# Eight transfers of the first steady unit on another queue, in an mLSTM and MLP kernel

## The chip, the cores and the metric

The kernel runs on one core of a Trainium2 chip. A core has five engines that run side by side and meet at semaphores: TensorE (PE in the profile; PEld is its weight load), VectorE (DVE), ScalarE (ACT), GpSimd (POOL) and SyncE (SP). SP, ACT and POOL can also start DMA transfers; each of them issues its own in the order of its instructions. The metric is the time of one execution in device microseconds (us).

## The reference, cut to what matters

```python
def _attn_ref(q, k, v, i_gate, f_gate, o_gate):          # B, H, S, D = 4, 8, 768, 40
    for t in range(S):
        m_new = np.maximum(f_gate[:, :, t] + m, i_gate[:, :, t])
        f_stab = np.exp(f_gate[:, :, t] + m - m_new)
        i_stab = np.exp(i_gate[:, :, t] - m_new)
        C = f_stab * C + i_stab * einsum('bhd,bhe->bhde', vt, kt)
        n = f_stab * n + i_stab * kt
        h_tilde = einsum('bhde,bhe->bhd', C, qt)
        denom = np.maximum(np.abs(einsum('bhd,bhd->bh', n, qt)), 1.0)
        y[:, :, t] = sigmoid(o_gate[:, :, t]) * h_tilde / denom
...
def _moe_ref(x, w_in, w_out):                             # x: 3072 x 320, d_ff 2048
    h = x @ w_in
    return (h - np.tanh(h)) @ w_out
```

A recurrent cell (mLSTM) with a state per head is followed by a two-layer MLP whose inner function is h - tanh(h). All is float32.

## The kernel before, in words

The sequence of 768 steps is cut into 6 chunks of 128. One chunk of one of the 4 batches is a unit, so there are 24 units, and two units make a group of 256 tokens for the MLP. The 2048 inner columns of the MLP are taken in 8 pairs of 128-wide blocks. A work item is one or two pairs of one group: first the products with `w_in` into the PSUM tiles `ph_up`, then the inner function on ACT and DVE (tiles `z`, `q`, `gt`), then the products with `w_out`. In the steady part these are done with seven products instead of eight on 2 by 2 blocks (`up_in_seven`, line 1220, `down_seven`, line 1029), which need sums and differences of blocks made beforehand: `sums_in` and `part` from `w_in` (`sum_w_in`, line 1196), `wT` from `w_out` (`sums_of_weights`, line 1005), `s` from `gt`. When a group's products with `w_out` are done, DVE puts the PSUM tiles `pS` together into the output tile `ob` (`put_together`, line 1072).

Units 0 to 5 are placed by a planner. Units 6 to 23 (`PLANNED = 6`, line 296) are the steady ones. Each runs as a chain over several engines: PE makes the scores (`ps`) and then the turned result `pT` (`block_turned`); ACT and DVE bring `pT` into `zt` (`turn_back`, line 905); four transfers write `zt` to device memory (`h_rows`), and four read it back in another order (`z_in`), the second four after the first have landed. Then DVE makes the denominator (`den`), scales by the output gate and has `y` (`ys`, `gate_turned`, line 928); DVE transposes it to `yt`, four transfers write it out (`y_rows`) and three on POOL's queue read it into `xT`, the MLP's input for that unit's group (`turn_by_store`, line 825). Of unit 6 the four `y_rows` transfers are on POOL's queue, of the other units on SP's.

Every engine's instructions are pinned to the order in which the program emits them (`class Pinned`, line 96), and a DMA is one of its issuing engine's instructions: whatever stands behind a waiting DMA waits too. What stands where is decided by the main loop: `spread_over` puts steps at fractional positions of the items (`START + x`), and `merge` (line 1375) lays them between PE's products. SP's queue also carries the copies of the recurrent states (`in_halves`, line 849, emitted ahead of the steady part) and the loads of the coming units (`load_unit`, line 355: `kz`, `qz`, `v`, `k`, `o`).

Of the kernel before, what the change touches and what calls it, by code (L numbers as in the profile page):

```python
# [79 lines left out]
def kernel(  # L80
# [33 lines left out]
    V, A, SP, G = Pinned(nc.vector), Pinned(nc.scalar), Pinned(nc.sync), Pinned(nc.gpsimd)  # L114
# [181 lines left out]
    PLANNED, LEFT = 6, 3  # L296
# [345 lines left out]
    part = [parts_of[n // GT][:, n % GT] for n in range(FIRST * GT)]  # L642
# [179 lines left out]
    BLOCK = 32  # L822
# [82 lines left out]
    def turn_back(n):  # L905


        t = un[n]
        both = att.tile([128, 2, HH * L // BLOCK, BLOCK], FP, name="zt", tag="P", bufs=4)
        zt, added = both[:, 0], both[:, 1].rearrange("p b i -> p (b i)")  # L910
        flat = zt.rearrange("p b i -> p (b i)")
        banks_of = [x.rearrange("p g t -> p (g t)") for x in t["turned"]]
        A.copy(out=added[:, HALF:], in_=banks_of[1][:, HALF:])
        V.transpose(flat[:, 0:HALF], banks_of[0][:, 0:HALF])
        sums = [x.rearrange("p (i t) -> p i t", i=2)[:, :, HALF:] for x in (added, banks_of[0])]
        V.tensor_tensor(out=sums[0], in0=sums[1], in1=sums[0], op=OP.add)
        V.transpose(flat[:, HALF:], added[:, HALF:])
        rows = dram.tile([2, 2, HH, L, BLOCK], FP, name="h_rows", tag=f"h_rows{n % 4}")
        for a in range(128 // BLOCK):
            half, low = divmod(a, 2)  # L920
            SP.dma_start(out=rows[low, half].rearrange("g (b k) i -> k (g b) i", k=BLOCK), in_=zt[a * BLOCK:(a + 1) * BLOCK])
        t["z"] = att.tile([L, 2, H, BLOCK], FP, name="z_in", tag="P", bufs=4)
        for i in range(4):
            part = slice(i * BLOCK, (i + 1) * BLOCK)
            SP.dma_start(out=t["z"][part].rearrange("t a h i -> t (a h) i"),
                         in_=rows.rearrange("a c g t i -> t (a c g) i")[part])

    def gate_turned(n):
# [215 lines left out]
    def up(some, shrink, quarters=False):  # L1144

        n = len(some)
        ph = [ps_h.tile([128, 2, TG], FP, name="ph_up", tag=f"ph{i}") for i in range(2)]

        def product(i, x, j):
            g, p = some[x]  # L1150
            f = 2 * p + i
            if j < NK:
                col = 2 * j + i
                lhs, rhs = w_in[:, p, col * 128:(col + 1) * 128], xT[slot_of(g)][:, j, :]
            else:
                rows = slice(i * HALF, (i + 1) * HALF)
                lhs, rhs = w_in[rows, p, 2 * NK * 128:], xT[slot_of(g)][rows, j, :]
            T.matmul(ph[i][:, x, :], lhs, rhs, start=(x == 0 and j == 0), stop=(j == NK), skip_group_check=True)

        def quarter(i, x, c):  # L1160
            g, p = some[x]
            rows, cols, first = slice(i * HALF, (i + 1) * HALF), slice(c * HALF, (c + 1) * HALF), 2 * NK * 128 + c * HALF
            T.matmul(ph[i][cols, x, :], w_in[rows, p, first:first + HALF], xT[slot_of(g)][rows, NK, :],
                     start=False, stop=True, skip_group_check=True)

        full = [(0.43, lambda i=i, x=x, j=j: product(i, x, j)) for i in range(2) for x in range(n) for j in range(NK)]
        if quarters:
            rest = [lambda i=i, x=x, c=c: quarter(i, x, c) for x in range(n) for c in range(2) for i in range(2)]
        else:
            rest = [lambda i=i, x=x: product(i, x, NK) for x in range(n) for i in range(2)]  # L1170
        return full, (rest, [lambda: shrink(some, ph)])
# [24 lines left out]
    def sum_w_in(p, E=V):  # L1196

        a11, a21, a12, a22 = (w_in[:, p, i * 128:(i + 1) * 128] for i in range(4))
        t = sums_in_of(p)
        both = w_in[:, p, 0:4 * 128].rearrange("p (j f) -> p j f", j=4)  # L1200
        return [lambda: E.tensor_tensor(out=t[:, 0:4:2], in0=both[:, 1:4:2], in1=both[:, 0:2], op=OP.subtract),
                lambda: E.tensor_tensor(out=t[:, 1], in0=a22, in1=t[:, 0], op=OP.subtract),
                lambda: E.tensor_tensor(out=t[:, 3], in0=a12, in1=t[:, 1], op=OP.subtract)]
# [196 lines left out]
    while sum(map(len, items)) < len(pairs):  # L1400
        x = sum(map(len, items))
# [64 lines left out]
    of_tokens, of_states, exponentials, rows = {}, {}, [], []  # L1466
# [252 lines left out]
    def spread_over(steps, x0, x1):  # L1719

        for i, (cost, step) in enumerate(steps):
            at = x0 + i * (x1 - x0) / len(steps)
            work[int(at)].append((at, cost, step))
# [9 lines left out]
    for i, slot in enumerate(slots):  # L1733
        x0, x1 = (START + max(0, 2 * j - 1) for j in (i, i + 1))
        begins[x0].append((slot, x0, x1))
    for p, x in enumerate((4.05, 6.05, 8.05, 2.02, 0.5, 0.8, 1.1, 1.4)):
        spread_over([(0.0, lambda step=step: step()) for step in sum_w_in(p, G)], START + x, START + x + 0.25)
    late = (4, 0.0, V), (5, 0.04, G), (6, 0.95, V), (7, 0.3, G)
    for p, x, E in (*late, *((p, x, G) for p, x in zip(order_of(FIRST)[:2] + order_of(FIRST)[-2:], (1.5, 1.75, 6.6, 7.5)))):
# [12 lines left out]
    for x in range(START, len(items) + LAG):  # L1752
# [17 lines left out]
        if x < len(items):  # L1770
            some = tuple(run[:2] for run in items[x])
            turned = [(1.9, lambda n=n: [block_turned(n), Clock.later("turned", 1.2, lambda: [turn_back(n), n + B < NU and keep_halves(n)])]) for n in scored]
            if x < len(items) - 1:
                plain = x < START + PLAIN
                if plain:
                    full, rest = up(some, shrink(x), bool(new[:1]))
                    dense = full[:4] + turned + full[4:]
                else:
                    stages, rest = up_in_seven(x, some)
                    dense = stages[0] + take(BETWEEN) + (turned if new else []) + stages[1] + take(BETWEEN) + stages[2]  # L1780
            else:
                dense, rest = up(some, shrink(x), bool(scored or new[:1]))
            dense.append((0.6 + 0.9 * len(new[:1]), lambda: halves(rest, *(crossed_scores(n) for n in new[:1]))))
            if x == len(items) - 1 or not new and not plain:
                dense += turned
# [96 lines left out]
    def shrink_any(ph):  # L1882
        z = mlp.tile([128, 2, TG], FP, name="z", tag="z")
        q = mlp.tile([128, 2, TG], FP, name="q", tag="q")
        t, big = (att.tile([128, 2, TG], FP, name=name, tag="P", bufs=4) for name in ("t", "big"))
        gt = mlp.tile([128, 2, TG], FP, name="gt", tag="gt", bufs=4)
        A.activation(out=z, in_=ph, func=AF.Square)
        A.activation(out=t, in_=ph, func=AF.Tanh)
        A.activation(out=q, in_=z, func=AF.Square, bias=square)
        A.activation(out=big, in_=z, func=AF.Relu, bias=border)  # L1890
        V.scalar_tensor_tensor(out=gt, in0=ph, scalar=lead, in1=z, op0=OP.mult, op1=OP.mult)
        V.tensor_tensor(out=t, in0=ph, in1=t, op=OP.subtract)
        V.scalar_tensor_tensor(out=gt, in0=z, scalar=root, in1=gt, op0=OP.add, op1=OP.mult)
        V.scalar_tensor_tensor(out=gt, in0=q, scalar=rest, in1=gt, op0=OP.add, op1=OP.mult)
        V.copy_predicated(gt, big.bitcast(I32), t)
        return gt

    with tc.If(loaded[0] > 0):
# [21 lines left out]
        for g in range(NG):  # L1920
# [19 lines left out]
            for p0 in range(0, NP, 2):  # L1940
                gts = []
                full, half = up(((g, p0), (g, p0 + 1)), lambda _, phs: gts.extend(shrink_any(ph) for ph in phs))
# [53 lines left out]
```

## Time and profile before

| | |
|---|---|
| Median of 3 timed runs | 501.25 us (500.5 to 503.71) |
| The profiled execution | 506.16 us, span 504.2 us |
| PE busy in the span | 489.6 us (97%) |
| DVE busy | 411.7 us (82%) |
| ACT busy | 268.8 us (53%) |
| POOL busy | 120.0 us (24%) |
| DVE idle until `z_in` landed, over the whole run | 8.3 us in 5 waits |

All times in what follows count from the start of the span. The page cuts the span into 40 slices, of 12.6 us each; a digit is the busy share in tenths. In rows of the order of time a row can be several instructions of one kind (x4); the first number is the start of the first, the second the time until the end of the last, and in brackets stands how long the engine had been idle and what ended that. Matmul rows overlap with the next, since matmuls are pipelined.

### The profile page before, as it was taken

The numbers are of one execution on the slowest core, as the hardware profiler recorded it, in microseconds if no ns is written. First come the engines' busy times: TensorE is split into PE (matmuls) and PEld (weight loads), VectorE is DVE, ScalarE is ACT, GpSimd is POOL, SyncE is SP. The second block draws the span as 40 slices with busy tenths as digits, with TensorE's granted clock in tenths as the row PEclk, the third lists the DMA queues.
The fourth block names the chain that finished last, engine by engine and source line by source line (L and its number), as shares of the span: only waits on it lengthen the run. The fifth ranks groups of instructions, "written<-read, shape, count | busy, mean of one in ns | idle before, by whom it ended". The sixth has DMA issues, their size and how long they took to land.

```text
span 504.2 us, 13823 instructions
## 1 busy us (share of the span) xinstructions
PE 489.6 (97%) x5208; PEld 438.3 (87%) x5208; DVE 411.7 (82%) x966; ACT 268.8 (53%) x729; POOL 120.0 (24%) x240
## 2 busy tenths in 40 slices
PE   9999999999699999999999999999999999999994
PEld 5778887779599989999999999999999999998984
DVE  4499898995699998887888888888888888885762
ACT  2788998534155445445455455455455464455540
POOL 4552343860134332102103103102102102111000
PEclk9999999999989999999999999999999999999998
DMA  7994395314255444454454344444344343320001
GB/s 226 276 268 128 106 145 151 95 41 89 46 146 119 89 113 80 96 134 89 94 123 98 82 121 85 96 119 96 76 111 101 66 114 59 59 62 10 27 2 31
DMA packets 144044, 51.26 MB, mean 102 GB/s; under 512 B 124004, under 2 KB 136484, under 8 KB 143972
## 3 DMA queue, kind: packets, MB, share of 16 engines
q1 hardware_dynamic: 135308, 31.70, 31.1%
q0 software_dynamic: 5184, 14.52, 9.6%
q10 hardware_dynamic: 3480, 4.10, 2.4%
q8 instruction: 43, 0.70, 0.6%
q14 instruction: 29, 0.24, 0.1%
HBM read 38.40 MB, written 11.60 MB: 99 GB/s over the span
## 4 chain that ended last, share of the span: by engine, by line
PE 81%; DVE 10%; DMA 3%; issue 2%; SPq 2%; ACT 1%; DVEq 0%; ACTq 0%
PE ph_up L129 34%; PE pS L129 29%; PE ps L129 4%; PE po L129 3%; PE pT L129 3%; PE awake L129 3%; PE ph L129 2%; DVE gt L106 2%; PE pc L129 2%; SPq L106 2%; DMA h_rows<-zt 1%; DMA z_in<-h_rows 1%; DVE s L106 1%; DMA y_rows<-yt 1%; DVE w_e L106 1%
## 5 line engine op out<-in xcount | busy, mean ns | idle before, releaser
L129 PE MATMUL ph_up<-xT,w_in 64*64 64x256 f32 (+3 forms) x1324 | 155.2, 349 | 0.2 <-DVE gt L106 0.2
L129 PEld LDWEIGHTS ph_up<-xT,w_in 128*128 128x128 f32 (+2 forms) x1324 | 114.2, 162 | 17.7 <-issue 3.3
L106 ACT ACTIVATE z<-ph_up 128x256 f32<-128x256 f32 (+1 forms) x98 | 40.7, 417 | 102.6 <-PE ph_up L129 80.8
L106 ACT COPY ph_up<-ph_up 128x256 f32<-128x256 f32 x117 | 41.8, 357 | 93.6 <-PE ph_up L129 62.9
L106 POOL DMA_DIRECT2D xT<-y_rows x54 | 31.7, 592 | 238.5 <-DMA y_rows<-yt 238.5
L129 PE MATMUL pS<-wT,s 128*128 128x160 f32 x504 | 87.2, 301 | 0.0
L129 PEld LDWEIGHTS pS<-wT,s 128*128 128x128 f32 x504 | 73.4, 192 | 0.3 <-issue 0.3
L106 ACT ACTIVATE q<-z,tiny 128x512 f32<-128x512 f32 (+1 forms) x98 | 68.9, 713 | 2.5
L106 DVE SCALAR_TENSOR_TENSOR gt<-q,gt 128x512 f32<-128x512 f32 (+1 forms) x98 | 66.6, 686 | 3.9 <-ACT q L106 1.5
L106 DVE TENSOR_TENSOR both<-ph_up,cs 128x256 f32<-128x256 f32 x78 | 32.7, 422 | 35.7 <-PE ph_up L129 30.4
L129 PE MATMUL pS<-w_out,gt 128*128 128x160 f32 x336 | 58.1, 316 | 3.2 <-DVE ob L106 3.2
L129 PEld LDWEIGHTS pS<-w_out,gt 128*128 128x128 f32 x336 | 47.8, 193 | 7.7 <-DVE ob L106 3.3
L129 PE MATMUL ph_up<-xT,sums_in 128*128 128x128 f32 x336 | 52.1, 278 | 1.0 <-DVE gt L106 1.0
L129 PEld LDWEIGHTS ph_up<-xT,sums_in 128*128 128x128 f32 x336 | 45.9, 193 | 1.9 <-issue 1.4
L129 PE MATMUL ph_up<-xT,part 128*128 128x128 f32 x288 | 44.7, 278 | 0.3 <-DVE gt L106 0.3
L106 DVE SCALAR_TENSOR_TENSOR gt<-ph_up,z 128x256 f32<-128x256 f32 (+1 forms) x98 | 41.2, 458 | 2.3 <-ACT z L106 2.2
L129 PEld LDWEIGHTS ph_up<-xT,part 128*128 128x128 f32 x288 | 38.9, 191 | 2.0 <-ACT ph_up L106 1.5
L106 DVE TENSOR_TENSOR s<-gt 128x256 f32<-128x256 f32 x84 | 34.1, 446 | 1.4
L129 PE MATMUL pS<-wT,gt 128*128 128x160 f32 x168 | 30.2, 303 | 0.0
L129 PE MATMUL pS<-w_out,s 128*128 128x160 f32 x168 | 29.7, 299 | 0.0
L129 PEld LDWEIGHTS ps<-qz,kz 40*64 40x64 f32 (+1 forms) x672 | 23.6, 148 | 5.6 <-issue 1.8
L129 PE MATMUL po<-w_out,gt 128*128 128x320 f32 x96 | 27.9, 439 | 0.0
(139 smaller groups left out, 747.7 us busy)
## 6 DMA issues: line engine op xcount, KB each, us to landing
w<-in_moe_w_out POOLq DMA_DIRECT2D x8, 640.0 KB, 5.4
h_rows<-zt SPq DMA_DIRECT2D x72, 64.0 KB
z_in<-h_rows SPq DMA_DIRECT2D x72, 64.0 KB
w<-in_moe_w_in POOLq DMA_DIRECT2D x16, 256.0 KB, 5.1
kz<-in_kT SPq DMA_DIRECT2D x48, 80.0 KB
o<-in_o_gate SPq DMA_DIRECT2D x24, 160.0 KB
qz<-in_qT SPq DMA_DIRECT2D x44, 80.0 KB
out<-ob ACTq DMA_DIRECT2D x11, 320.0 KB
```

The source lines that it names most:

```text
L106: i = method(*args, **kwargs)
L129: return cls.keep(nc.tensor.matmul(*args, **kwargs))
```

## The change

Two things change. In `turn_back` the eight transfers of unit 6, `h_rows` and `z_in`, are issued by POOL instead of SP. And the three sums of `w_in` for pair 7 start at position 1.3 instead of 1.4, so that they come ahead of these transfers in POOL's order.

```diff
         V.transpose(flat[:, HALF:], added[:, HALF:])
+        queue = G if n == PLANNED else SP
         rows = dram.tile([2, 2, HH, L, BLOCK], FP, name="h_rows", tag=f"h_rows{n % 4}")
         for a in range(128 // BLOCK):
             half, low = divmod(a, 2)
-            SP.dma_start(out=rows[low, half].rearrange("g (b k) i -> k (g b) i", k=BLOCK), in_=zt[a * BLOCK:(a + 1) * BLOCK])
+            queue.dma_start(out=rows[low, half].rearrange("g (b k) i -> k (g b) i", k=BLOCK), in_=zt[a * BLOCK:(a + 1) * BLOCK])
         t["z"] = att.tile([L, 2, H, BLOCK], FP, name="z_in", tag="P", bufs=4)
         for i in range(4):
             part = slice(i * BLOCK, (i + 1) * BLOCK)
-            SP.dma_start(out=t["z"][part].rearrange("t a h i -> t (a h) i"),
+            queue.dma_start(out=t["z"][part].rearrange("t a h i -> t (a h) i"),
                          in_=rows.rearrange("a c g t i -> t (a c g) i")[part])
...
-    for p, x in enumerate((4.05, 6.05, 8.05, 2.02, 0.5, 0.8, 1.1, 1.4)):
+    for p, x in enumerate((4.05, 6.05, 8.05, 2.02, 0.5, 0.8, 1.1, 1.3)):
         spread_over([(0.0, lambda step=step: step()) for step in sum_w_in(p, G)], START + x, START + x + 0.25)
```

On SP, behind the loads of unit 8 (`o` is the last of them) and ahead of those of unit 9 (which begin with `kz`), the transfers of unit 6 (numbers 1304 and 1309) and of unit 7 (1499 and 1504) follow each other. This is the difference in SP's order, with the tiles' numbers:

```order
 L106 DMA k_1236<-in_k 64x160 x2
 L106 DMA o_1241<-in_o_gate 128x320
-L106 DMA h_rows_1304<-zt_1299 32x16x32 x4
-L106 DMA z_in_1309<-h_rows_1304 32x16x32 x4
 L106 DMA h_rows_1499<-zt_1494 32x16x32 x4
 L106 DMA z_in_1504<-h_rows_1499 32x16x32 x4
```

Unit 6's eight transfers have left; unit 7's stand directly behind the loads of unit 8.

On POOL, at the end of the sums of `w_in` for pairs 4 to 7 (`sums_in`), this stood before; `wT` are the sums of `w_out` for pairs 0 and 3, `part_148` those of `w_in` for pair 3, and `vs` is the clearing of unit 7's spare columns:

```order
L106 MEMSET vs 128x23
L106 TENSOR_TENSOR sums_in<-w_in,sums_in 128x128
L106 TENSOR_TENSOR wT<-w_out 128x160
L106 TENSOR_TENSOR sums_in<-w_in,sums_in 128x128
L106 TENSOR_TENSOR wT<-w_out,wT 128x160
...
L106 TENSOR_TENSOR wT<-w_out,wT 128x160
L106 TENSOR_TENSOR part_148<-w_in 128x2x128
L106 TENSOR_TENSOR part_148<-w_in,part_148 128x128 x2
L106 DMA y_rows<-yt 32x10x32 x4
```

And this stands there now:

```order
L106 TENSOR_TENSOR sums_in<-w_in,sums_in 128x128 x2
L106 MEMSET vs 128x23
L106 DMA h_rows<-zt 32x16x32 x4
L106 DMA z_in<-h_rows 32x16x32 x4
L106 TENSOR_TENSOR wT<-w_out 128x160
...
L106 TENSOR_TENSOR wT<-w_out,wT 128x160
L106 TENSOR_TENSOR part_148<-w_in 128x2x128
L106 TENSOR_TENSOR part_148<-w_in,part_148 128x128 x2
L106 DMA y_rows<-yt 32x10x32 x4
```

The last sums of pair 7 come ahead of the transfers; all eight sums `wT` of pairs 0 and 3 and the three of `part_148` now stand behind them, ahead of unit 6's `y_rows` as before.

## The prediction

> **What bounds the kernel now.** I read the page first: who is busy, and where the busiest engine is not.
>
> ```profile
> span 504.2 us, 13823 instructions
> ...
> PE 489.6 (97%) x5208; PEld 438.3 (87%) x5208; DVE 411.7 (82%) x966; ACT 268.8 (53%) x729; POOL 120.0 (24%) x240
> ...
> PE   9999999999699999999999999999999999999994
> ```
>
> PE is busy in 97% of the span, so time is won only where PE waits or runs slowly. Apart from the last slice there is one such slice, the eleventh (126.1 to 138.7 us). The order of time on PE shows what happens there:
>
> ```profile
> 130.01 1.63 PE L129 MATMUL ph_up<-xT,w_in 128*128 128x128 f32 x20
> 133.00 1.17 PE L129 MATMUL ps<-qz,kz 40*64 40x128 f32 x32 [1.36 <-issue]
> 137.38 2.50 PE L129 MATMUL pS<-w_out,gt 128*128 128x160 f32 x8 [3.21 <-DVE ob L106]
> 141.83 1.19 PE L129 MATMUL ph_up<-xT,sums_in 128*128 128x128 f32 x4
> 143.42 0.98 PE L129 MATMUL pS<-wT,s 128*128 128x160 f32 x6
> ```
>
> Two pauses, 1.36 and 3.21 us. From the last products of one item (130.01) to the first `s` products inside the next (143.42) it takes 13.41 us. The same passage comes again at the next two ends of a group:
>
> ```profile
> 156.90 1.64 PE L129 MATMUL ph_up<-xT,w_in 128*128 128x128 f32 x20
> 162.81 0.98 PE L129 MATMUL pS<-wT,s 128*128 128x160 f32 x6
> ...
> 176.29 1.64 PE L129 MATMUL ph_up<-xT,w_in 128*128 128x128 f32 x20
> 181.95 0.68 PE L129 MATMUL ph_up<-xT,sums_in 128*128 128x128 f32 x4 [0.98 <-DVE gt L106]
> 182.91 0.98 PE L129 MATMUL pS<-wT,s 128*128 128x160 f32 x6
> ```
>
> There it takes 5.91 and 6.62 us. The first passage thus loses 7.50 or 6.79 us against its like. Of 7.50, 4.57 are the two pauses; the other 2.93 are slow products, and the table by stretches shows why (columns: busy of PE, PEld, DVE, ACT, POOL, then the granted clock):
>
> ```profile
> 135.00:136.00 1.00, 0.00 (x0) 0.00 (x0) 0.97 (x3) 0.00 (x0) 0.00 (x0) 1.00 0.12 16
> 137.00:138.00 1.00, 0.61 (x2) 0.62 (x3) 0.93 (x3) 0.00 (x0) 0.75 (x2) 0.50 0.44 66
> 143.00:144.00 1.00, 1.00 (x10) 1.00 (x9) 1.00 (x3) 0.44 (x3) 1.00 (x5) 0.93 0.67 158
> ```
>
> After the pauses the clock is at 0.50, and is back by 144. Both pauses wait for DVE, so DVE comes next:
>
> ```profile
> 112.27 0.65 DVE L106 STREAM_TRANSPOSE zt<-zt 128x448 f32<-128x448 f32 x1
> ...
> 129.53 0.17 DVE L106 SCALAR_TENSOR_TENSOR den<-z_in,inv 128x8 f32<-128x8 f32 x1 [6.21 <-DMA z_in<-h_rows]
> 132.39 0.52 DVE L106 TENSOR_TENSOR zt<-pT,zt 128x384 f32<-128x384 f32 x1
> 136.88 0.45 DVE L106 TENSOR_TENSOR ob<-pS,a 128x320 f32<-128x320 f32 x1
> 140.94 0.75 DVE L106 SCALAR_TENSOR_TENSOR gt<-ph_up,z 128x256 f32<-128x256 f32 x2
> ```
>
> DVE stood still from 123.32 to 129.53 for unit 6's `z_in`, and then caught up. In its order behind `den` come all that PE waited for: `zt` of unit 7, whose reading of `pT` frees the banks for `ps`; `ob`, which frees `pS`; `gt<-ph_up`, which frees `ph_up` for the products of 141.83. Unit 6's own `zt` was ready at 112.92. Why did `z_in` need until 129.5? SP's order of time answers:
>
> ```profile
> 111.58 3.71 SPq L106 DMA_DIRECT2D state<-state  x5
> ...
> 120.45 0.58 SPq L106 DMA_DIRECT2D o<-in_o_gate  x1
> 121.13 3.02 SPq L106 DMA_DIRECT2D h_rows<-zt  x4
> 125.83 1.90 SPq L106 DMA_DIRECT2D z_in<-h_rows  x4
> 133.61 2.82 SPq L106 DMA_DIRECT2D h_rows<-zt  x4
> 138.14 1.92 SPq L106 DMA_DIRECT2D z_in<-h_rows  x4
> ...
> 149.32 1.97 SPq L106 DMA_DIRECT2D y_rows<-yt  x4
> ```
>
> SP was still issuing state copies and unit 8's loads, and came to `h_rows` at 121.13: 8.21 us of the 16.6 from `zt` to `den` are waiting in SP's order.
>
> **The change part by part.** POOL at that time:
>
> ```profile
> 102.01 0.57 POOL L106 TENSOR_TENSOR wT<-w_out 128x160 f32<-128x160 f32 x1
> ...
> 108.31 1.11 POOL L106 TENSOR_TENSOR part<-w_in,part 128x128 f32<-128x128 f32 x2
> 137.25 2.41 POOL L106 DMA_DIRECT2D y_rows<-yt  x4 [27.83 <-DVE yt L106]
> 142.09 1.77 POOL L106 DMA_DIRECT2D xT<-y_rows  x3 [2.42 <-DMA y_rows<-yt]
> ...
> 153.10 1.79 POOL L106 DMA_DIRECT2D xT<-y_rows  x3 [6.95 <-DMA y_rows<-yt]
> ```
>
> *The eight transfers.* POOL is idle from 109.42 to 137.25, so `h_rows` goes out as soon as `zt` is there, at 112.92. The trace shows neither `h_rows` nor `z_in` on POOL, so their time comes from neighbours. `y_rows`, also four transfers, shows both routes, from first issue until its reader runs: 3.78 us on SP (149.32 to 153.10), 4.84 on POOL (137.25 to 142.09). POOL's route adds 1.06. `h_rows` took 4.53 on SP (133.61 to 138.14), so 5.59 on POOL; `z_in` took 3.70 (125.83 to 129.53), so 4.76. It lands at 112.92 + 5.59 + 4.76 = 123.27, just when DVE is free for it (123.32). Bounds: if the route's addition is nothing, 121.2, which gains no more, since DVE is busy; if it is doubled, 125.4.
>
> The Trainium skill ("DMA: Bandwidth & Descriptors", section "Issuing engine by pattern") speaks against this move: simple loads and stores belong on Sync, whose path is called generally faster. The trace agrees on the direction, with 1.06 us per stage, 2.1 for both; by the rule alone the sum would be a loss of 2.1 us, but it leaves out the 8.21 us in SP's order.
>
> *From DVE to PE.* With `den` at 123.4, everything behind it moves by 6.13. Its inputs are there: the last that it reads, the `pS` products under `ob`, stand in PE's order ahead of the row at 130.01. `ph_up<-xT,sums_in` came 12.30 us after `den` (129.53 to 141.83), DVE being busy nearly all the while; now that is 135.70. PE's own products reach that point a little earlier (20 products from 130.01, then `ps` and 16 `pS`, unhindered), so DVE still sets it, as at 181.95. From there to the `s` products it is 0.96 (181.95 to 182.91) at full clock: 136.66 instead of 143.42. That is **6.76 us won**, and lies between the two comparisons above (6.79 and 7.50) and the stall alone (6.21). Pauses of under 1 us remain; the one of 0.98 left the products behind it at their usual pace, so I count no slow clock. Next late is DVE's `gt`, as at the other two ends.
>
> *The sums behind the transfers.* POOL issues until about 118.5 + 2.4 = 120.9 (`z_in` on SP waits for `h_rows` in the same way; four issues on POOL took 2.41). The eight `wT` and three `part` sums, until now from 102.01 to 109.42, then run from 120.9 to about 128. Nobody waits for them: the earliest reader are the `part` products at 161.84, some 27 us later even after the shift.
>
> ```profile
> 125.76 0.61 PE L129 MATMUL ph_up<-xT,sums_in 128*128 128x128 f32 x4
> ...
> 161.84 0.68 PE L129 MATMUL ph_up<-xT,part 128*128 128x128 f32 x4 [0.27 <-DVE gt L106]
> ```
>
> `y_rows` of unit 6 comes at about 131, behind them as before. But they now run beside DVE's work after `den` instead of its work before `zt`, and the two disturb each other:
>
> ```profile
> 105.77 1.87 DVE L106 SCALAR_TENSOR_TENSOR gt<-q,gt 128x512 f32<-128x512 f32 x2
> 115.63 1.28 DVE L106 SCALAR_TENSOR_TENSOR gt<-q,gt 128x512 f32<-128x512 f32 x2
> ...
> 95.80 1.31 POOL L106 TENSOR_TENSOR sums_in<-w_in 128x256 f32<-128x256 f32 x1
> 98.80 0.74 POOL L106 TENSOR_TENSOR sums_in<-w_in 128x256 f32<-128x256 f32 x1
> ```
>
> A `gt<-q,gt` took 0.30 us more beside POOL's sums. Between 123.4 and 128 DVE has three of that size and some smaller ones: 0 to 1.2 us, I take **0.6 lost**, half. What is won before `zt`, for the same reason, makes `h_rows` earlier by up to a microsecond; that only secures the landing.
>
> *The sums of pair 7, a little sooner*, cost nothing: the same three instructions, around 102, read by the `sums_in` products from 125.76 on. Without this they would wait behind the transfers. *On SP* unit 7's `h_rows` now wait at the head of the queue for their `zt`, as before; unit 9's loads move with it.
>
> **Sum**: 6.76 - 0.6 = 6.16. The profiled execution would go from 506.16 to 500.0; its span of 504.2 to 498.0. The runs' median is 4.91 below the profiled execution, which I take to be outside this passage; from 501.25 the forecast is 495.1. One per cent, 5.0 us, is about what a measurement can tell from no change.
>
> **The rivals.** *The transfers land late, or the loss is smaller without a profile.* Transfers: if all eight issues are stretched as the POOL sum above (0.74 to 1.31, about twice), that is 8 times 0.60 more, and `z_in` lands at 128.1: 1.4 us won, 499.9; between this and the forecast lie gains of 2 to 5. For it speaks that loads of unit 8 move at the same time. The loss: the three timed runs spread over 3.21, about the 2.93 of the slow clock, so the median run may not have had it, and gains 3.2: 498.0. Both together 0.28, with 496.3 to 499.
>
> *Nothing won*: another wait ends last at `den`, or a later stage takes it back. Against it stands the list of PE's waits (in total, times, longest):
>
> ```profile
> PE ph_up L129 <- DVE gt L106: 1.5, 3, 1.0
> ```
>
> Two of the three are the rows at 161.84 and 181.95; nothing longer waits behind 144 that could take the gain back. 0.08, with 499 to 502.
>
> *Slower: POOL's issue is held up by DVE.* Should each of the eight issues take three times 0.60, `z_in` lands 9.6 later, at 132.9, 3.4 behind today: 504.6. It decides against the change from 1.37 us per issue on (8 times 0.77 = the 6.2 in hand). Against it: `y_rows` on POOL took 0.60 per issue in 137 to 139, where DVE was 0.93 busy with the same kinds of instruction. 0.04. The Trainium skill ("SBUF — State Buffer", section "SBUF: two separate sides") states such a mechanism: GpSimd cannot write its descriptors while DVE runs certain two-port instructions, such as a float32 copy. DVE's rows quoted here hold none of these, and the 0.60 beside 0.93 agrees; no run here shows the held case.
>
> **How the numbers follow.** Forecast 0.60 (gain 5 to 8: 493.2 to 496.2), late or smaller 0.28, nothing 0.08, slower 0.04. The range from 493.2 (7.50 and 0.5 of eased DVE work) to 498.9 takes in the first two and leaves out about 0.15. Faster by over 1% (under 496.2): 0.60; slower by over 1% (above 506.3): 0.03, the far end of the last rival; else 0.37.
>
> **What would show it.** In the changed profile: POOL issues `h_rows` at 111.5 to 113 and `z_in` about 5.6 later; `den` starts at 123.4, with less than 1 us idle before it; the passage on PE from the 20 products to the `s` products takes 6 to 7.5 us instead of 13.4; the clock stays at 1.00; the eleventh slice becomes a 9; `gt<-q,gt` behind `den` is 0.2 to 0.3 longer. I am wrong if `den` still waits over 2 us, if POOL's issues are over 1 us each, or if the passage is short and the time unchanged.

## The result and the profile after

The changed kernel takes 493.35 us in the median of six runs (492.58 to 494.77), the kernel before, timed beside it, 500.93 (500.5 to 503.71): a ratio of 0.984, 95% interval 0.9813 to 0.9867. That is 7.58 us less, where 6.15 were forecast, and close to the lower end of the forecast's range (493.2). It is more than the 1% that was taken as what a measurement can tell, on the side that had 0.60. A ratio is worked out from the single runs, leaving out those more than 1.5% above the kernel's fastest, and so is not quite the quotient of the two medians.

The page of the changed kernel, the same lines as quoted of before (the span, the busy times, PE's 40 slices):

```profile
span 490.9 us, 13826 instructions
...
PE 480.2 (98%) x5208; PEld 432.5 (88%) x5208; DVE 409.8 (83%) x966; ACT 268.9 (55%) x729; POOL 125.3 (26%) x248
...
PE   8999999999899999999999999999999999999995
```

The eleventh slice is an 8, no longer a 6. PE's order of time in the passage, from the last 20 products of an item to the first products with `s` in the next:

```profile
123.59 1.64 PE L129 MATMUL ph_up<-xT,w_in 128*128 128x128 f32 x20
125.05 0.85 PE L129 MATMUL ps<-qz,kz 40*64 40x128 f32 x32
...
130.20 0.68 PE L129 MATMUL ph_up<-xT,sums_in 128*128 128x128 f32 x4 [1.77 <-DVE gt L106]
...
131.16 0.98 PE L129 MATMUL pS<-wT,s 128*128 128x160 f32 x6
```

It takes 7.57 us instead of 13.41. Both pauses are gone (before `ps`, and the one for `ob`), a new one of 1.77 has come, and the products run at their full pace (`ps` in 0.85 instead of 1.17). POOL and DVE, in the same stretch:

```profile
105.75 2.61 POOL L106 DMA_DIRECT2D h_rows<-zt  x4 [8.38 <-DVE state L106]
110.74 2.57 POOL L106 DMA_DIRECT2D z_in<-h_rows  x4 [2.39 <-DMA h_rows<-zt]
...
117.44 0.73 POOL L106 TENSOR_TENSOR part<-w_in 128x256 f32<-128x256 f32 x1
118.25 1.45 POOL L106 TENSOR_TENSOR part<-w_in,part 128x128 f32<-128x128 f32 x2
```

```profile
104.81 0.65 DVE L106 STREAM_TRANSPOSE zt<-zt 128x448 f32<-128x448 f32 x1
...
116.16 0.75 DVE L106 SCALAR_TENSOR_TENSOR gt<-ph_up,z 128x256 f32<-128x256 f32 x2
116.83 0.20 DVE L106 SCALAR_TENSOR_TENSOR den<-z_in,inv 128x8 f32<-128x8 f32 x1
117.06 0.46 DVE L106 TENSOR_TENSOR den<-den,z_in 128x8 f32<-128x8 f32 x1
117.55 0.20 DVE L106 RECIPROCAL den<-den 128x8 f32<-128x8 f32 x1
117.67 1.05 DVE L106 SCALAR_TENSOR_TENSOR gt<-q,gt 128x512 f32<-128x512 f32 x1
```

`h_rows` is issued 0.3 us after `zt` (105.46), and `den` follows DVE's other work without a wait, where it stood 6.21 us before. But `gt<-q,gt` behind it takes 1.05 us beside POOL's `part` sums. In the kernel before, the same instruction behind `den`, with POOL idle, took 0.64:

```profile
130.06 0.64 DVE L106 SCALAR_TENSOR_TENSOR gt<-q,gt 128x512 f32<-128x512 f32 x1
```

**The two profiled spans differ by 13.3 us, the medians by 7.6.** 5.4 of the difference (17.27 less 11.90, where the last rows below end) is not the change's: in the profiled execution of before, PE's first products run at half pace. The kernel before (columns as above):

```profile
6.08 2.37 PE L129 MATMUL ps<-qz,kz 40*128 40x128 f32 x16
...
13.54 3.73 PE L129 MATMUL awake<-diag 128*128 128x512 bf16 x9
```

and the same rows of the changed one:

```profile
5.94 1.16 PE L129 MATMUL ps<-qz,kz 40*128 40x128 f32 x16
...
9.78 2.12 PE L129 MATMUL awake<-diag 128*128 128x512 bf16 x9
```

The granted clock reads 1.00 in both. Such a start comes and goes with the execution: a second profile of the kernel before (e1, below) began at full pace, and one of the changed kernel with a delay (e12) at half. The comparisons below therefore go by stretches, and for the whole by the second profile.

### The profile page after: what moved, and what is told of

The parts are those of the page before. It is cut to its first block, busy times and chain, and to the rows that moved or that the text cites. A ratio compares the mean times of both kernels' runs of the same rounds, so it can differ in the third digit from the quotient of the medians.

```text
span 490.9 us, 13826 instructions
## 1 busy us (share of the span) xinstructions
PE 480.2 (98%) x5208; PEld 432.5 (88%) x5208; DVE 409.8 (83%) x966; ACT 268.9 (55%) x729; POOL 125.3 (26%) x248
## 4 chain that ended last, share of the span: by engine, by line
PE 89%; DVE 7%; issue 2%; ACT 1%; DMA 0%; SPq 0%; ACTq 0%; DVEq 0%
PE ph_up L129 39%; PE pS L129 31%; PE po L129 5%; PE pT L129 4%; PE ps L129 3%; PE pc L129 2%; PE ph L129 2%; DVE gt L106 1%; PE awake L129 1%; DVE ob L106 1%; DVE s L106 1%; ACT z L106 1%; DMA w_out<-in_i_gate 0%; DVE both L106 0%; PE px L133 0%
## 5 line engine op out<-in xcount | busy, mean ns | idle before, releaser
L129 PE MATMUL pS<-w_out,gt 128*128 128x160 f32 x336 | 56.9, 312 | 0.0
L129 PEld LDWEIGHTS pS<-w_out,gt 128*128 128x128 f32 x336 | 46.8, 189 | 4.4 <-issue 1.9
L106 DVE TENSOR_TENSOR s<-gt 128x256 f32<-128x256 f32 x84 | 33.1, 434 | 1.4
L106 DVE SCALAR_TENSOR_TENSOR gt<-both,z 128x512 f32<-128x512 f32 x39 | 26.6, 683 | 0.0
```

The costliest lines, as they stand in the source:

```text
L106: i = method(*args, **kwargs)
L129: return cls.keep(nc.tensor.matmul(*args, **kwargs))
```

## The experiments

Twelve kernels were timed and profiled, in three groups (e1 to e4, e5 to e8, e9 to e12). The kernels of a group share the runs of the kernel before that were timed beside them, with medians of 502.04, 501.47 and 501.56 us. The intervals of the ratios are up to 1.3% wide, so most of what follows rests on the profiles.

The passage is always the one shown above; "the end" is from the last four products `pS` to the end of the span; DRAIN is the longest of the three instructions of that name that POOL has at the end of the program, of which more below.

| kernel | `den` waits | passage | end | DRAIN | time | ratio to before |
|---|---|---|---|---|---|---|
| before | 6.21 | 13.41 | 7.66 | 8.24 | 500.93 | |
| changed | 0 | 7.57 | 6.18 | 2.36 | 493.35 | 0.984 (0.9813 to 0.9867) |
| e1, before again | 5.96 | 12.54 | 7.60 | 8.24 | 501.42 | 0.9973 (0.9929 to 1.0016) |
| e2, sums only | 6.12 | 13.45 | 7.62 | 8.24 | 501.75 | 0.9987 (0.9937 to 1.0037) |
| e3, queue only | 0 | 7.81 | 6.18 | 2.36 | 494.99 | 0.9857 (0.9793 to 0.992) |
| e4, loads later | 0.60 | 7.16 | 7.66 | 8.24 | 495.68 | 0.9843 (0.9777 to 0.9908) |
| e5, changed again | 0 | 7.61 | 6.18 | 2.36 | 493.67 | 0.9864 (0.9809 to 0.992) |
| e6, sums later | 0 | 6.45 | 6.25 | 2.36 | 497.9 | 0.9918 (0.9877 to 0.9959) |
| e7, e4 and eight more | 0.53 | 7.07 | 6.59 | 2.36 | 494.36 | 0.9851 (0.9824 to 0.9878) |
| e8, delay of ten fills | 3.21 | 12.05 | 5.68 | 2.36 | 496.68 | 0.9901 (0.9884 to 0.9919) |
| e9, part sum sooner | 0 | 6.84 | 5.82 | 2.36 | 494.12 | 0.9876 (0.983 to 0.9922) |
| e10, before and eight more | 5.71 | 12.28 | 5.93 | 2.36 | 499.6 | 0.9968 (0.9931 to 1.0005) |
| e11, before and four more | 5.76 | 12.32 | 5.90 | 1.22 | 498.14 (one run) | |
| e12, delay of four fills | 1.13 | 8.97 | 5.81 | 2.36 | 496.38 | 0.9872 (0.9816 to 0.9929) |

The theory after the result: the gain is the landing of `z_in` in time, which came of the place in SP's order; POOL's queue as such adds nothing. The first rival: it is POOL's queue, or the sums, that won. The second: part of it was won elsewhere.

### The parts of the change, and the place on SP (e1 to e4)

e1 is the kernel before, unchanged.

> The kernel before, unchanged, profiled and timed once more. It tells how much of the difference between the two profiles (spans of 504.2 and 490.9, 13.3 us) belongs to the kernel. Theory A: of the 13.3 us some 5.4 lie ahead of 24 us (PE products at half pace in the first 12 us of the profile of before) and 1.5 behind the last products; both are of the execution, not of the kernel, so a second profile of before may start at full pace, and then has a span of about 499, with the passage from the 20 products ahead of ps to the s products again at 13 to 13.5 us and DVE idle about 6 us ahead of den. Theory B: start and end belong to the kernel; the span is 504 again. Timed against before: 1.000 within 0.3%.

e2 has only the number of the sums:

```diff
-    for p, x in enumerate((4.05, 6.05, 8.05, 2.02, 0.5, 0.8, 1.1, 1.4)):
+    for p, x in enumerate((4.05, 6.05, 8.05, 2.02, 0.5, 0.8, 1.1, 1.3)):
```

> Only the earlier sums of pair 7 (1.3 instead of 1.4), all transfers on SP. Theory A: no difference, ratio 1.000 within 0.3%, passage 13 to 13.5 us. Rival: a part of the unexpected size of the gain (7.6 us timed against 6.2 forecast) comes from here: 1 to 2 us faster.

e3 has only the queue:

```diff
+        queue = G if n == PLANNED else SP
-            SP.dma_start(out=rows[low, half]...
+            queue.dma_start(out=rows[low, half]...
-            SP.dma_start(out=t["z"][part]...
+            queue.dma_start(out=t["z"][part]...
```

> Only the queue of unit 6's eight transfers, sums of pair 7 left at 1.4, so that the last of them stands behind the transfers and one wT sum on POOL. Theory A: as the whole change, ratio 0.982 to 0.988, passage 7 to 8 us; the last sum comes at about 114.5 and is first read behind 120. Rival: PE waits for that sum, and 1 us or more of the gain is missing.

e4 leaves the eight transfers on SP and puts the loads of unit 8 behind them:

```diff
-            if s + 1 < NU and s + 1 not in ld:
+            late_loads = s == PLANNED + 1
+            if s + 1 < NU and s + 1 not in ld and not late_loads:
                 load_unit(s + 1, ("kz", "qz", "v", "k", "o"), crossed=True)
...
+        if s == PLANNED + 1:
+            steps.append((0.0, lambda: load_unit(s + 1, ("kz", "qz", "v", "k", "o"), crossed=True)))
         steps.append((0.0, lambda: [gates.extend(gate_turned(o)), gates[0]()]))
```

> The transfers stay on SP, but the loads of unit 8 (9.0 us of its order up to 121) are emitted behind unit 6's h_rows and z_in instead of ahead of them; the state copies stay ahead. POOL keeps its order apart from one memset. Theory A, that the place in SP's order was the cost and POOL's queue itself gives nothing: h_rows goes out when the state copies end, about 2.4 us behind zt instead of 8.2; z_in lands about 10.7 us behind zt, as it was forecast for POOL; DVE waits 0 to 1 us; ratio 0.984 to 0.988. Since the wT sums stay ahead of zt, DVE's way from den to gt should take 12.3 us as before, not 13.4. Rival, that SP's issue is slow there or the state copies were the real wait: DVE waits 3 us or more and the gain is under 4 us (ratio above 0.992).

The sums win nothing that can be measured (e2), the queue alone brings `den` without a wait (e3, passage 7.81). The second profile of before (e1) starts at full pace, with a span of 498.5, and confirms the wait at `den`; its passage, from the first to the last PE row here, is 12.54, a little under the 13 to 13.5 expected:

```profile
124.82 1.64 PE L129 MATMUL ph_up<-xT,w_in 128*128 128x128 f32 x20
137.36 0.98 PE L129 MATMUL pS<-wT,s 128*128 128x160 f32 x6
```

```profile
124.10 0.17 DVE L106 SCALAR_TENSOR_TENSOR den<-z_in,inv 128x8 f32<-128x8 f32 x1 [5.96 <-DMA z_in<-h_rows]
```

SP's order in e4, then its `den`:

```profile
98.49 10.85 SPq L106 DMA_DIRECT2D state<-state  x14
109.44 2.04 SPq L106 DMA_DIRECT2D h_rows<-zt  x4
113.00 1.90 SPq L106 DMA_DIRECT2D z_in<-h_rows  x4
114.94 0.79 SPq L106 DMA_DIRECT2D kz<-in_kT  x2
```

```profile
117.96 0.17 DVE L106 SCALAR_TENSOR_TENSOR den<-z_in,inv 128x8 f32<-128x8 f32 x1 [0.60 <-DMA z_in<-h_rows]
```

On SP, behind the state copies but ahead of the loads, the transfers do as well: `den` waits 0.60, and the passage is 7.16. Of the 8.21 us in SP's order the loads, some 5.7 (115.33 to 120.45 and the last one's 0.58; not 9.0, as expected), were what counted; the copies ahead cost what is left of the wait. From `den` to `ph_up` it takes 12.29 us in e4, as before, for POOL's `wT` and `part` sums stay ahead of `zt` there.

SP is the faster way all the same. From the first `h_rows` to the `den` that waits for `z_in` it takes 8.29 to 8.80 us in the seven profiles with these transfers on SP (8.52 in e4), and 9.76 (e8) and 11.32 (e12) in the two with them on POOL in which `den` waits. The rule of the Trainium skill weighed in the prediction, plain transfers on Sync ("DMA: Bandwidth & Descriptors", section "Issuing engine by pattern"), agrees with that; it says nothing of the place in the order, which decided.

Yet e4's span was 492.5 and its end 7.66 us, against 6.18 of the changed kernel. That end was the next question.

### The end of the program (e5, e7, e10, e11)

The changed kernel again, to see what returns:

> The changed kernel once more, word for word, so that what is told of it rests on two profiles. If its four differences from the kernel before belong to the change and not to one execution, they come again within 0.1 to 0.2 us: z_in's last issue ended near 113.3 and den taken up without a wait; from the last product with x20 to the first product with s 7.6 us (7.57 there), with one pause of 1.8 us until gt; gt<-q,gt at 1.05 us; from the last products pS to the end of the span 6.2 us (6.18), against 7.6 to 7.7 in the kernel before, with GpSimd's last DRAIN at 2.36 us against 8.24. Time 493.4 us. Rival: the short end was this execution's own; then the end comes at 7.6 us here and the time stays 493.4, since the timed runs held both kinds.

All four returned: 7.61, no wait, 1.05 for `gt<-q,gt`, 6.18 at the end. e7 is e4 with eight transfers more on POOL, four units later; e10 and e11 are the kernel before with the same eight, or with four:

```diff
+        if n == PLANNED + 4:
+            spare = dram.tile([2, 2, 2, HH, L, BLOCK], FP, name="spare", tag="spare")
+            for a in range(8):
+                half, low = divmod(a % 4, 2)
+                G.dma_start(out=spare[a // 4, low, half].rearrange(...), in_=zt[(a % 4) * BLOCK:(a % 4 + 1) * BLOCK])
```

> The kernel with the transfers of unit 6 back on SP and unit 8's loads behind them (profiled before at 492.5 us, 7.66 us of them from the last products pS to the end, with a last DRAIN of 8.24 us on GpSimd), and with eight transfers more in GpSimd's queue four units later: a second copy of zt to a place in memory that nothing reads. Theory (the number of transfers that GpSimd issued sets how long its last DRAIN takes): the DRAIN is 2.4 us as in the changed kernel, the end 6.2 us, the span 491.1 and the time 494.2 or less. Rival: the end hangs on which transfers these are, or on their moment; then the DRAIN stays at 8.24 us, the end at 7.66, the time at 495.7. Four units later GpSimd has room: the eight issues take 5.2 us there (8 x 0.65) and should cost nothing on PE; if they do, PE's pauses in that unit show it.

> The kernel before, with eight transfers more in GpSimd's queue some four units behind the place of the change (a second copy of zt to a place in memory that nothing reads), and nothing else. Theory (the number of transfers in GpSimd's queue sets its last DRAIN): DRAIN 2.4 us instead of 8.24, from the last products pS to the end 6.2 to 6.6 us instead of 7.6 to 7.7, the time 1.0 to 1.4 us less than the kernel before, 500.1 against 501.4, a ratio of 0.997 to 0.998; den's wait (6.0 us) and the passage (12.5 to 13.5) stay. Rival: the shorter end belongs to the kernels whose h_rows moved in time; then DRAIN stays at 8.24 and the ratio at 1.000.

> The same with four transfers more instead of eight. If the DRAIN grows or falls with each transfer, it lies between 8.24 and 2.36 us, near 5.3. If it is a matter of a full or an empty rest (a count in steps), it is 8.24 or 2.36 and nothing between. No reading for the time.

The rows show the end of the program by line (POOLq and SPq: instructions of those engines that aren't counted as work; columns: count, then shortest, median and longest in ns, first and last start in us). The kernel before:

```profile
L1992 POOLq EVENT_SEMAPHORE  x4: 17/17/17, 503.4 to 504.1; - x4
L1992 POOLq DRAIN  x3: 40/107/8240, 495.1 to 503.9; - x3
L1992 SPq DRAIN  x3: 7/7/7, 501.5 to 503.6; - x3
```

The changed kernel:

```profile
L1993 POOLq EVENT_SEMAPHORE  x4: 17/17/17, 490.1 to 490.8; - x4
L1993 POOLq DRAIN  x3: 46/103/2355, 483.3 to 490.6; - x3
L1993 SPq DRAIN  x3: 7/7/7, 490.0 to 490.3; - x3
```

e10, then e11:

```profile
L1997 POOLq DRAIN  x3: 40/170/2360, 489.1 to 496.3; - x3
```

```profile
L1997 POOLq DRAIN  x3: 40/107/1217, 489.1 to 495.8; - x3
```

POOL begins the first of its three DRAINs some 1.4 us ahead of PE's last four products (496.54 in before, 484.72 after). I take it for the longest, since 8.24 us from the last start would go past the end of the span. At 8.24 us it ends at 503.35 (495.1 + 8.24), 1.85 us after SP was ready at 501.5, and the program ends with it. At 2.36 us it is over at 485.7, long before SP (490.0), and costs nothing. e10 shows that the number of transfers in POOL's queue does it: nothing else was changed, `den` still waits 5.71 us, and the DRAIN is 2.36, the end 5.93. The time is 499.6 against 501.56; the interval of the ratio reaches just past 1 (1.0005), so the gain at the end is shown by the profile and only likely by the time. In e7 the DRAIN fell as well, and the end from 7.66 to 6.59; its ratio (0.9851) doesn't differ from e4's (0.9843), so there the time doesn't confirm it. e11 fits neither thing expected of it: four transfers more give 1.22, eight 2.36, none 8.24, so the DRAIN neither falls nor rises throughout. From four to eight it grows by 0.29 us per transfer (1.14 over 4), and by that rate 8.24 would stand for 29 transfers; a count that starts anew somewhere between none and four more would fit. That is an estimate from three values; what the DRAIN waits for was not shown.

### What POOL's sums cost beside DVE (e6, e9)

e6 puts the eight `wT` and three `part` sums later:

```diff
-    for p, x in enumerate((4.05, 6.05, 8.05, 2.02, 0.5, 0.8, 1.1, 1.3)):
+    for p, x in enumerate((4.05, 6.05, 8.05, 4.07, 0.5, 0.8, 1.1, 1.3)):
...
-    ... zip(order_of(FIRST)[:2] + order_of(FIRST)[-2:], (1.5, 1.75, 6.6, 7.5)))):
+    ... zip(order_of(FIRST)[:2] + order_of(FIRST)[-2:], (4.12, 4.15, 6.6, 7.5)))):
```

> The changed kernel, with GpSimd's sums of w_out of two pairs and of one part of w_in taken out of the stretch in which VectorE works from den to ys, and put some 10 us later. Theory (contention): they lengthened gt<-q,gt from 0.64 to 1.05 us, o from 0.49 to 0.74, ys from 0.42 to 0.56, and with them the way from den to the first ph_up of the next unit from 12.30 to 13.37 us. Gone, this way is 12.3 to 12.5 us again, PE's one pause ahead of the products with s falls from 1.77 to 0.7 us, the passage from 7.57 to 6.5, the time to 492.4 us. Rival: the longer way comes of the transfers in GpSimd's queue, not of the sums; then gt<-q,gt stays at 1.0 us, the way at 13.3 and the time at 493.4. Second rival: the sums cost as much in their new place (GpSimd comes later to xT of unit 7 or holds VectorE there), the passage is shorter and the time isn't.

Where they were taken away, the theory holds to the tenth: `gt<-q,gt` takes 0.64, `den` to `ph_up` 12.25 instead of 13.37, and the pause is 0.81, the passage 6.45. But the second rival was right about the whole: 497.9, 4.2 slower than the changed kernel beside it (e5). The loss lies behind the passage, where it takes 359.54 us to the last products `pS`, 5.98 more than in the changed kernel. DVE a unit later, then PE:

```profile
132.06 0.66 DVE L106 TENSOR_TENSOR den<-den,z_in 128x8 f32<-128x8 f32 x1
132.76 0.20 DVE L106 RECIPROCAL den<-den 128x8 f32<-128x8 f32 x1
132.88 6.02 DVE L106 SCALAR_TENSOR_TENSOR gt<-q,gt 128x512 f32<-128x512 f32 x1
138.93 0.97 DVE L106 TENSOR_TENSOR s<-gt 128x256 f32<-128x256 f32 x2
```

```profile
143.87 1.19 PE L129 MATMUL ph_up<-xT,sums_in 128*128 128x128 f32 x4 [3.17 <-DVE gt L106]
```

One `gt<-q,gt` takes 6.02 us instead of 0.64, during which POOL works off sums of two kinds turn about, one starting every 0.4 to 0.5 us. Why it stood so long was not shown. e9 moves only the `part` sums, and to before `h_rows`:

```diff
-    for p, x in enumerate((4.05, 6.05, 8.05, 2.02, 0.5, 0.8, 1.1, 1.3)):
+    for p, x in enumerate((4.05, 6.05, 8.05, 1.3, 0.5, 0.8, 1.1, 1.3)):
```

> The changed kernel, with the part sum of w_in of pair 3 (2.2 us on GpSimd, one of 0.73 and two of 0.73) made some 20 us sooner, in the 8.4 us in which GpSimd stood idle ahead of h_rows. The eight sums of w_out stay behind z_in and end near 117.7, when den has been taken up. Theory (contention by GpSimd's sums beside VectorE's reading): gt<-q,gt behind den, which ran beside the part sums, falls from 1.05 to 0.65 us, o from 0.74 to 0.49 and ys from 0.56 to 0.42; the way from den to the next ph_up from 13.4 to 12.5 to 12.8 us, PE's pause from 1.8 to 0.9 to 1.2, the passage from 7.6 to 6.7 to 7.0; ahead of it VectorE loses at most 0.4 in the sums' new place, so the time is 492.9 to 493.3 us against 493.4 to 493.7 of the changed kernel. Rival (contention only moves): what the passage wins, VectorE loses ahead of zt, and the 20 products come as much later; then the time is 493.5. Second rival, from the kernel with all the sums put later: two sums taken turn about on GpSimd hold VectorE for microseconds (there one instruction stood 6.02 us); here the part sum takes turns with the last sums of w_in, from 96 to 100, and PE would pause there; then the time is 496 or more.

```profile
117.57 0.28 DVE L106 SCALAR_TENSOR_TENSOR den<-z_in,inv 128x8 f32<-128x8 f32 x1
...
118.49 0.64 DVE L106 SCALAR_TENSOR_TENSOR gt<-q,gt 128x512 f32<-128x512 f32 x1
```

`gt<-q,gt` is back at 0.64 and the passage at 6.84, as the theory says. But from PE's first `ps` to the `s` products it is 125.33 (5.85 to 131.18) against 125.22 (5.94 to 131.16): what the passage won (0.73) was lost ahead of it (0.84). As far as one profile shows it, the first rival holds, contention only moves; the times (494.12 against 493.35 and 493.67) can't tell the two kernels apart. The second rival failed: POOL made `part` and `sums_in` turn about from 95.52 to 98.95, PE's only pause behind that was 0.28, and the longest row of DVE beside them is 1.28 us for two instructions. So two kinds of sums turn about do not by themselves hold DVE for microseconds, and the 6.02 of e6 has a further condition that no run here isolates. The Trainium skill ("GPSIMD Engine Reference", section "1. Specifications") says that GpSimd's access to SBUF is shared with VectorE and contended by its instructions with two SBUF inputs. `gt<-q,gt` reads two such tiles and grew by 0.41 us; the size, up to the 6.02 of e6, only the traces give.

### How late the transfers may land (e8, e12)

Both are the changed kernel with this ahead of `h_rows` on POOL, ten fills in e8 and four in e12:

```diff
+        if n == PLANNED:
+            G.tensor_copy(out=diag[:, 1, 0:BLOCK], in_=zt[:, 0])
+            for _ in range(10):
+                G.memset(diag[:, 1:5], 0.0)
```

> The changed kernel with a copy from zt and ten fills of a dead tile on GpSimd ahead of its h_rows transfers: some 5 to 6 us during which its queue stands (10 x 0.53 by the sums of that size, and the copy). Theory (only the moment of landing counts, and the changed kernel has about half a microsecond to spare: the last part of z_in issued by 112.7 lands by 116.2 and den is taken up at 116.83): den waits for z_in 4.7 to 5.5 us, the passage grows from 7.57 to 11.5 to 12.8 us and the time to 497.6 to 498.6. Rival (the place in line on SP was not what held the kernel before; its gain came from GpSimd's queue as such): den waits as long and the time stays below 495. Second rival: the spare time is larger, some 2 us, since the pause of 1.77 us that is left hides the sums behind it; then the time is 496.

> The changed kernel with the copy from zt and four fills of a dead tile on GpSimd ahead of h_rows: by the fills of the kernel with ten (5.76 us for ten, 0.58 each, and 4.62 us later at h_rows, since the first 1.2 us fell into the wait for zt) h_rows comes 1.1 to 1.3 us later. There, den waited 3.21 us of 4.62: 1.4 us to spare. If this holds, den waits 0 here, the passage stays at 7.6 us and the time at 493.4 to 493.7 us; if each microsecond of delay costs its share (no spare time, the sums behind it meet VectorE later), the time is 494.5 or more.

`z_in` in the changed kernel, e8 and e12, in this order (first and last start of its issues, then the time to landing):

```profile
L106 POOL DMA_DIRECT2D z_in<-h_rows x4: 649/649/652, 110.7 to 112.7; - x4
...
DMA to landing us min/median/max: 3.5/3.5/3.7
```

```profile
L106 POOL DMA_DIRECT2D z_in<-h_rows x4: 649/649/652, 115.8 to 117.7; - x4
...
DMA to landing us min/median/max: 2.4/2.4/2.5
```

```profile
L106 POOL DMA_DIRECT2D z_in<-h_rows x4: 649/649/649, 117.2 to 119.1; - x4
...
DMA to landing us min/median/max: 3.2/3.6/4.3
```

In e8, `h_rows` came 4.62 us later behind `zt`, `den` waited 3.21, the passage grew by 4.48 and the time to 496.68, 3.0 more than e5 beside it:

```profile
120.21 0.28 DVE L106 SCALAR_TENSOR_TENSOR den<-z_in,inv 128x8 f32<-128x8 f32 x1 [3.21 <-DMA z_in<-h_rows]
```

The gain does hang on the moment of landing, though the wait and the time stayed below the 4.7 to 5.5 and 497.6 to 498.6 expected. Not all of the 4.48 is the wait: `den` to `ph_up` takes 14.35 us in e8 (120.21 to 134.56), 0.98 more than in the changed kernel, since more of POOL's sums run beside DVE's work there. From 4.62 less 3.21 I read 1.4 us to spare, and e12 shows that this was wrong: 1.14 us later behind `zt`, and `den` already starts 1.13 us late, the passage grows by 1.40. (The profile puts that wait down to nothing it shows; by the rows the last part of `z_in` landed at 119.1 + 4.3 = 123.4, and `den` started at 123.50.) The rows settle it: in the changed kernel the last part lands by 112.7 + 3.7 = 116.4, and `den` is taken up at 116.83, so some 0.4 us are to spare. In e8, `z_in` landed 1.1 us faster than that, so its wait was that much shorter; in e12 it landed up to 0.6 us slower, which is a part of its 1.13. e12's time says nothing: its four runs lie between 492.85 and 499.45, and the profiled one, the longest, began at half pace.

## Where the prediction failed, and what of it held

**The step that failed is the sum.** It took the passage on PE for the whole of the gain, and put at nothing what the change does ahead of the passage and at the end of the program. Against e1, which like the changed kernel starts at full pace, the spans differ by 7.6 us (498.5 less 490.9), and this is where they lie:

| | e1 | changed | won | in the sum |
|---|---|---|---|---|
| from PE's first `ps` to the 20 products | 118.74 | 117.65 | 1.09 | 0 |
| the passage | 12.54 | 7.57 | 4.97 | 6.16 |
| from its end to the last `pS` | 353.54 | 353.56 | -0.02 | 0 |
| the end | 7.60 | 6.18 | 1.42 | 0 |
| the first `ps` | 6.08 | 5.94 | 0.14 | 0 |

- *The end of the program* had no term. POOL's DRAIN ended last there, at 503.4, and eight transfers more in POOL's queue made it short enough to hide: 1.42 us. The prediction costed each queue that the transfers pass, and not what their number does at the program's end; and it took the last slice, in which PE stands at 4 tenths, for granted.
- *"What is won before `zt` ... only secures the landing."* It reached PE: the 20 products came 1.09 us sooner. Part of it are short pauses: 0.21 ahead of `ph_up` and 0.16 ahead of `ps` in the profile of before, 0.17 in e1, none in the changed kernel; the rest is spread and wasn't taken apart. That it comes of POOL's sums, gone from beside DVE, is borne out by the other profiles that start at full pace: with all the sums in their old place this stretch takes 118.30 to 118.95 us (e1, e2, e4, e7, e10, e11), with the sums behind the transfers or later 117.65 to 118.11 (changed, e3, e5, e6, e8). The step took a shift on DVE for slack, where PE waited for DVE in the same stretch.
- *"I take 0.6 lost"* by the sums behind the transfers: `den` to `ph_up` grew from 12.30 to 13.37, so 1.07, near the bound of 1.2. It stands in the passage's 4.97, and leaves a pause of 1.77 where pauses of under 1 us were forecast (0.81 in e6, without these sums). This and the term before it are one thing: the sums cost about 1 us in either place (for the `part` sums alone, e9 shows it).
- *The passage* was to take 7.25 after the change (13.41 less 6.16) and took 7.57. The other 0.87 of what it won less is that the passage of e1 is shorter than that of the profile forecast from (12.54 against 13.41).

The forecast of 495.1 lay 1.75 above the time, 1.4 of it the end. That it came so near is in part luck: the 1.19 that the passage won less and the 1.09 won ahead of it nearly cancel.

**What held.** SP's order was the cause, `z_in` the wait, DVE's order behind `den` what PE paused for: e3 and e4 show it from two sides, and e8 brings the wait back. `den` came without a wait (forecast: less than 1 us); the stage from `h_rows` to `z_in` took 4.99 (forecast 5.59). Against the profile of before, the passage shrank by 5.84, where 6.16 were forecast. The sums of pair 7 cost nothing and won nothing (e2). The 4.91 between profiled execution and median did lie outside the passage, in the half-pace start: from the first `ps` to the 20 products that execution takes 123.93 us, 5.19 more than e1. Of the rivals, late landing and a held issue didn't occur: the issues took 0.65 us each, far from the 1.37 that would decide. That the passage could lose less in another execution was right as far as e1 goes, and not by the 2.9 us of the slow clock.

**Of the list of signs**, the granted clock stayed at 1.00 through the passage, as forecast (0.50 behind the pauses of before). `gt<-q,gt` behind `den` was to grow by 0.2 to 0.3 and grew by 0.41. The eleventh slice was to be a 9 and is an 8, for the pause of 1.77; the passage of 7.57 lies just past the 6 to 7.5 named.

## What to carry to other kernels

Where a transfer is late, look first at what its issuing engine has in order ahead of it: here, putting the loads behind it on the same queue brought the same passage as a second queue, within half a microsecond (7.16 and 7.57). Work of GpSimd beside VectorE isn't free cover, and moving it moved the cost (e9) or made it larger (e6). Look at the program's end as well, at which engine's DRAIN ends last: here the number of transfers in GpSimd's queue changed it by up to 7 us, of which the end of the program felt 1.4 to 1.7.

## What the runs showed of the hardware that was not expected

- GpSimd's DRAIN at the end took 8.24 us in four profiles without added transfers on its queue, 2.36 with eight more in nine, 1.22 with four more in one; only the 8.24 ended last.
- One VectorE instruction of 0.64 us stood 6.02 us while GpSimd ran two kinds of sums turn about (e6); beside sums of one kind it took 1.05. In e9, beside two kinds turn about, the longest row is 1.28 for two instructions, so what made the 6.02 is open.
- The same four `z_in` transfers landed 2.4 us after issue in e8 and 3.2 to 4.3 in e12. The share of the DMA engines in use was 0.29 to 0.47 in the microseconds behind their last issues in e8, 0.82 to 0.92 in e12; SP issued the loads of unit 8 from 109.7 to 115.4 in e8, ahead of `z_in`, and from 116.0 to 121.7 in e12, beside it. That the loads are the cause is argued, not shown.
- PE's products up to some 17 us ran at half pace in two of the profiles (before and e12; 2.37 and 2.08 us for 16 `ps` against 1.16), with a granted clock of 1.00 in the profile of before, and about 5 us went with it. What starts it was not shown.
